# Attention and expert layer on one core: v's blocks turned by the DMA engines instead of TensorE, from the seventh step on

## The chip, the cores and the metric

The kernel runs on one core of a Trainium2 chip. Its engines are TensorE (PE in the profile; PEld is its loading of weights), VectorE (DVE), ScalarE (ACT), GpSimd (POOL) and SyncE (SP), each with an instruction queue of its own that is worked off in order; 16 DMA engines move data between the chip's HBM and the on-chip memory SBUF. Matmuls write to PSUM. The metric is the device time of one execution in microseconds (us), the median of several runs.

## The reference

Four batches of `q`, `k`, `v`, each 5056 tokens by 256 channels in fp32, go through an attention over channels, and all 20224 tokens then through a layer of 8 experts of which each token takes one:

```
qn = q / (norm over tokens + 1e-6);  kn = k / (norm over tokens + 1e-6)
a  = softmax(kn^T @ qn / tau)                     # 256 x 256, one per batch
x  = v @ a                                        # 20224 x 256
e  = argmax(x @ w_gate + modality_bias[modality_id])
p  = the softmax's value at e
out[token] = p * (relu(x[token] @ w1[e]) @ w2[e]) # w1[e] 256 x 1024, w2[e] 1024 x 256
```

## The kernel before, in words

A batch is cut into 10 steps of 512 tokens (the last has 448), so there are 40 steps, numbered g. Per step the kernel does this:

- `va_pieces`: it loads the step's `v` (one transfer of 512 KB, partition p taking four neighbouring tokens), turns it so that channels lie on partitions, splits it in a high part `vh` and a low part `vl`, and multiplies it with the batch's `a` and with `a @ w_gate` in one go (`av`: six matmuls for each of four groups of 128 tokens, tiles `xp`, copied to `x` by ScalarE). `route` works out the expert of each token on VectorE (tiles L, mx, lm, val, vm, oh, run), counts rows per expert by three small matmuls into `rp`, and gives each token a row number; `send` scatters the tokens' rows into the list `xs` in HBM through GpSimd's indirect transfers.
- `kq_pieces`: it loads `q` and `k` of the next batch and adds to that batch's 256 x 256 matrix (matmuls `g`), and sums squares for the norms (tiles `sq`, added to `acc`).
- `block_pieces`: it takes 512 rows of one expert out of `xs` (`xr`), turns them on TensorE (`xtp`), and runs both expert matrices over them (matmuls `hp`, relu into `hh` and its remainder `hl`, matmuls `y`), with weights loaded in halves (`w1r`, `w2r`) and split in high and low parts. The first such block is loaded in step 5 and runs beside step 6; from then on about one block goes with each step, and some are left for after the last step.

Each exact product is made of three matmuls on split operands. All are issued by `_interleave`, which deals the pieces of the three streams out evenly over a step; a scheduler then sets the order on each queue, and pools of buffers (the number of buffers is the number in the pool's name, or `bufs`) decide what has to wait for a release. All plain loads are issued by SP's queue, in order. A transfer on SP waits in that queue until its buffer is free, and whatever is behind it waits too.

The part that the change touches is `tr(h)` (L519 to L531), for each half h of the channels: four transposes on TensorE against the identity `ident` (L524) fill a PSUM tile `vtp`, ScalarE casts it to `vh` (L528), VectorE subtracts to get `vl` (L529). The steps g < 6 are called early; they run before the first block. `first_block` is 6. The pieces `tr(0)`, `tr(1)` of step g + 1 are dealt out at the start of step g, ahead of that step's own `av` and `route`.

Of the kernel before, what the change touches and what calls it, by code (L numbers as in the profile page):

```python
# [8 lines left out]
F32 = mybir.dt.float32  # L9
F32R = mybir.dt.float32r  # L10
BF16 = mybir.dt.bfloat16
I32 = mybir.dt.int32
AF = mybir.ActivationFunctionType
ALU = mybir.AluOpType
# [20 lines left out]
def kernel(  # L35
# [47 lines left out]

    HELD = {1: 3, 2: 2}

    def parts(s):
# [34 lines left out]
        pattern=[[N, B], [STEP, NS], [1, TT]],  # L121
# [92 lines left out]
    def turn_mod():  # L214
# [7 lines left out]
            raw[:R, 0 : 2 * STEP].rearrange("r (p t w) -> r t p w", t=TT, w=2)[:, :, :, 0],  # L222
# [34 lines left out]
    def kq_pieces(b, s, behind=(), later=None):  # L257
# [51 lines left out]
        def square(h):  # L309
            ts = slice(2 * h, 2 * h + 2)  # L310
            a = acc[b]
            for n, o in (("q", 0), ("k", C)):
                first = h == 0 and s == 0
                sq = a[:, :, o : o + C]
                if not first:
# [4 lines left out]
                    if b == 0 or (b == 1 and s < AHEAD):  # L320
                        sq = p3.tile([P, 2, C], F32, tag="hh" if n == "q" else "hl", name=f"sq_{b}_{s}_{h}_{n}")
                    else:
                        sq = p2.tile([P, 2, C], F32, tag="sq", name=f"sq_{b}_{s}_{h}_{n}")
# [36 lines left out]
    def softmax_pieces(b):  # L360
# [27 lines left out]
        def soft(m):  # L388
            rq, rk, ae = st["rq"], st["rk"], st["ae"]
            sc = p1.tile([P, C], F32, tag="sc", name=f"sc_{b}_{m}", bufs=2)  # L390
# [95 lines left out]
    first_block = LAG + START  # L486

    def va_pieces(b, s):
        pp = parts(s)
# [4 lines left out]

        def fetch():
            if "v" in st:
                return
            vt = p2.tile([P, TT, C], F32, tag="v", name=f"v_{g}")
            if pp < P:
                z0 = pp // 32 * 32  # L500
                nc.vector.memset(vt[z0:], 0.0)
            nc.sync.dma_start(
                vt[:pp], v[b, t0 : t0 + pp * TT, :].rearrange("(p t) c -> p t c", t=TT)
            )
            st["v"] = vt

        def load():
            fetch()
# [7 lines left out]
        def tr(h):  # L516
            if early and h == 1:
                tp = ps1.tile([P, 512], F32, tag="y1", name=f"vtp_{g}_{h}")
            else:  # L519
                tp = ps2.tile(  # L520
                    [P, 512], F32, tag="h" if early else "aux", name=f"vtp_{g}_{h}", bufs=2 if early else 3
                )
            for t in range(TT):
                nc.tensor.matmul(  # L524
                    tp[:, t * P : (t + 1) * P], st["v"][:, t, h * P : (h + 1) * P], ident,
                    is_transpose=True, start=t == 0, stop=True, skip_group_check=True,
                )
            cast[g] = nc.scalar.copy(st["vh"][:, h, :], tp).ins  # L528
            ins = nc.vector.tensor_tensor(st["vl"][:, h, :], tp, st["vh"][:, h, :].bitcast(F32), ALU.subtract)  # L529
            if g == 0:  # L530
                order(ins.ins, [i for _, i in weighted])  # L531
# [16 lines left out]
        def route():  # L548
# [19 lines left out]

            W = TT * E
# [6 lines left out]
            else:  # L576
                rp = ps2.tile([P, 512], F32, tag="aux", bufs=3, name=f"rp_{g}")
            nc.tensor.matmul(rp[:, 0:W], trim[:pp], ohf[:pp], start=True, stop=False, skip_group_check=True)
            nc.tensor.matmul(rp[:, 0:W], onesb[:pp], rtf[:pp], start=False, stop=True, skip_group_check=True)
            nc.tensor.matmul(  # L580
                rp[:, W : W + E], onesb[:pp], run_t[:pp, :, TT - 1], start=False, stop=True, skip_group_check=True
# [25 lines left out]
        def send(behind=()):  # L607
            pi, x = st["pi"], st["x"]
            for t in range(TT):
                ins = scatter(  # L610
# [8 lines left out]
            [load] + [lambda h=h: tr(h) for h in range(CH)],  # L619
            [lambda t=t: av(t) for t in range(TT)] + [route],  # L620
            fetch,
# [283 lines left out]
    va = [va_pieces(*divmod(g, NS)) for g in range(G)]  # L905
    run(va[0][0])
# [7 lines left out]
    for g in range(G):  # L914
        b, s = divmod(g, NS)
        streams = []
        if g == first_block - 1:
            va[g + 1][2]()
            va[g + 2][2]()
# [8 lines left out]
        if g - 1 in HELD:  # L928
            t = HELD[g - 1]
            own.insert(t + 1, lambda: va[g - 1][3]([copied[g, t]]))  # L930
        streams.append(soft + (va[g + 1][0] if g + 1 < G else []) + own)
# [107 lines left out]
```

## Time and profile before

| | |
|---|---|
| median of 3 runs | 1235.48 us (1234.66 to 1236.76) |
| the profiled execution's own time | 1232.32 us |
| its span | 1230.5 us |
| mean clock granted to TensorE | 0.996 |
| TensorE busy | 1212.9 us, 99% of the span |
| VectorE busy | 828.8 us, 67% |
| ScalarE busy | 735.6 us, 60% |
| GpSimd busy | 345.6 us, 28% |
| moved by the DMA engines | 210.83 MB, 171 GB/s on average |

The profile shows one execution. Times in it count from the span's start. A line of its groups names the source line, the engine, the operation, out<-in by the tiles' names, the number of instructions, their busy time and the mean length of one; what follows the second bar is the idle time of the engine just before them. In a timeline each row has start, length, engine, line and operation, and in square brackets the idle time before it and what ended that. TensorE's instructions overlap, so the time that one costs is the distance from its start to the next one's start, not its length.

### The profile page before, as it was taken

The page shows a single profiled execution, that of the slowest core. Times are in us where ns is not written, and L with a number is a line of the kernel's source. Part 1 is how long each engine was busy: PE and PEld are TensorE (multiplying, and loading weights), DVE is VectorE, ACT ScalarE, POOL GpSimd, SP SyncE. Part 2 cuts the span into 40 slices and gives each one's busy share as a digit, 9 for nine tenths or more (in the row PEclk, how much of TensorE's full clock was granted, in tenths as well). Part 3 has the DMA queues.
Part 4 walks back from the last instruction along what each step waited for, and adds up shares of the span by engine and source line. Part 5 has one row for each costly group of instructions (what it writes and reads, how often), then busy time and mean ns, then how long its engine had stood idle before and what let it go on. Part 6 is the DMA issues. An engine that isn't in the chain of part 4 may idle for free.

```text
span 1230.5 us, 23793 instructions
## 1 busy us (share of the span) xinstructions
PE 1212.9 (99%) x8368; PEld 1116.1 (91%) x8368; DVE 828.8 (67%) x2182; ACT 735.6 (60%) x1511; POOL 345.6 (28%) x344
## 2 busy tenths in 40 slices
PE   8989999999999999999999999999999999999997
PEld 7888999999999999999999999999999999999996
DVE  6788687877677766776676776666556665575552
ACT  6666676866666665766666665555555555545552
POOL 0061432122322323213222223222222232243121
PEclk9999999999999999999999999999999999999998
DMA  8988555555555655545555564435544554444330
GB/s 306 297 274 281 157 201 171 192 173 174 180 182 173 182 177 174 180 151 181 174 179 184 169 182 147 138 122 154 171 148 142 172 153 138 128 154 146 117 99 29
DMA packets 104177, 210.83 MB, mean 171 GB/s; under 512 B 11336, under 2 KB 52808, under 8 KB 104048
## 3 DMA queue, kind: packets, MB, share of 16 engines
q1 hardware_dynamic: 88304, 167.61, 43.9%
q0 software_dynamic: 15744, 41.61, 9.2%
q8 instruction: 67, 1.10, 0.4%
q14 instruction: 62, 0.51, 0.2%
HBM read 167.06 MB, written 43.43 MB: 171 GB/s over the span
## 4 chain that ended last, share of the span: by engine, by line
PE 86%; issue 7%; DMA 3%; POOL 1%; DVE 1%; ACT 1%; SPq 0%; POOLq 0%; DVEq 0%; ACTq 0%
PE hp L780 32%; PE y L800 32%; PE xp L542 9%; PE g L345 7%; PE vtp L524 3%; PE xtp L761 2%; DMA k<-in_k_dram 2%; POOL out_dram L457 1%; DMA q<-in_q_dram 1%; DMA xs<-x,pi 1%; DMA xr<-xs 0%; PE gw L417 0%; PE ns L367 0%; PE ns L372 0%; SPq L284 0%
## 5 line engine op out<-in xcount | busy, mean ns | idle before, releaser
L800 PE MATMUL y<-w2h,hh 128*128 128x256 f32 x1256 | 355.3, 283 | 0.0
L800 PE MATMUL y<-w2l,hh 128*128 128x256 f32 x1256 | 350.3, 279 | 0.0
L800 PE MATMUL y<-w2h,hl 128*128 128x256 f32 x1256 | 348.7, 278 | 0.1
L457 POOL DMA_INDIRECT out_dram<-yo,xr x158 | 157.2, 995 | 513.3 <-ACT hh L783 400.3
L457 POOL DMA_INDIRECT xs<-x,pi x160 | 175.8, 1099 | 344.4 <-ACT w1h L740 129.1
L784 DVE SCALAR_TENSOR_TENSOR hl<-hp,hh 128x512 fp32r<-128x512 f32 (+1 forms) x320 | 216.4, 676 | 72.5 <-ACT hh L783 72.3
L780 PE MATMUL hp<-xh,w1h 128*128 128x512 f32 (+1 forms) x640 | 255.0, 399 | 0.0
L780 PE MATMUL hp<-xh,w1l 128*128 128x512 f32 (+1 forms) x640 | 250.7, 392 | 0.0
L780 PE MATMUL hp<-xl,w1h 128*128 128x512 f32 (+1 forms) x640 | 250.5, 392 | 0.0
L800 PEld LDWEIGHTS y<-w2h,hh 128*128 128x128 f32 x1256 | 236.0, 188 | 11.0 <-ACT yo L815 0.4
L800 PEld LDWEIGHTS y<-w2l,hh 128*128 128x128 f32 x1256 | 236.5, 188 | 9.6
L783 ACT ACTIVATE hh<-hp 128x512 fp32r<-128x512 f32 (+1 forms) x320 | 190.1, 594 | 83.3 <-PE hp L780 78.0
L800 PEld LDWEIGHTS y<-w2h,hl 128*128 128x128 f32 x1256 | 235.2, 187 | 0.3 <-DVE hl L784 0.3
L747 DVE TENSOR_TENSOR w1l<-w1r,w1h 128x512 fp32r<-128x512 f32 x160 | 110.1, 688 | 173.2 <-ACT w1h L740 171.2
L740 ACT CAST w1h<-w1r 128x512 fp32r<-128x512 f32 x160 | 100.1, 626 | 146.5 <-PE hp L780 143.2
L780 PEld LDWEIGHTS hp<-xh,w1l 128*128 128x128 f32 x640 | 120.5, 188 | 26.2
L780 PEld LDWEIGHTS hp<-xl,w1h 128*128 128x128 f32 x640 | 120.7, 189 | 14.7 <-DVE xl L768 0.4
L780 PEld LDWEIGHTS hp<-xh,w1h 128*128 128x128 f32 x640 | 120.4, 188 | 12.8
L740 ACT CAST w2h<-w2r 128x512 fp32r<-128x512 f32 x160 | 101.2, 632 | 47.9 <-PE y L800 47.7
L747 DVE TENSOR_TENSOR w2l<-w2r,w2h 128x512 fp32r<-128x512 f32 x160 | 109.8, 686 | 23.9 <-ACT w2h L740 21.9
L546 ACT COPY x<-xp 128x264 f32<-128x264 f32 x160 | 61.0, 382 | 81.7 <-PE xp L542 74.6
L542 PE MATMUL xp<-ah,vh 128*128 128x264 f32 x320 | 92.3, 289 | 0.4 <-DVE vl L529 0.4
(153 smaller groups left out, 1712.4 us busy)
## 6 DMA issues: line engine op xcount, KB each, us to landing
w1r<-in_moe_w_dram SPq DMA_DIRECT2D x80, 512.0 KB, 4.1
w2r<-in_moe_w_dram SPq DMA_DIRECT2D x80, 512.0 KB, 3.8
xr<-xs SPq DMA_DIRECT2D x38, 516.0 KB, 4.6
v<-in_v_dram SPq DMA_DIRECT2D x36, 512.0 KB, 3.5
q<-in_q_dram SPq DMA_DIRECT2D x35, 512.0 KB, 6.0
k<-in_k_dram SPq DMA_DIRECT2D x35, 512.0 KB, 6.4
xs<-x,pi POOLq DMA_INDIRECT x160, 5.0
out_dram<-yo,xr POOLq DMA_INDIRECT x158, 3.2
```

Source lines behind the costliest of these rows:

```text
L345: nc.tensor.matmul(gram[b][:, m, :], x, y, start=first and m == 0 and i == 0, stop=last and i == len(seq) - 1, skip_group_check=True,)
L457: ins = nc.gpsimd.indirect_dma_start(out=dst, out_offset=bass.IndirectOffsetOnAxis(ap=idx, axis=0), in_=rows, in_offset=None, bounds_check ...
L524: nc.tensor.matmul(tp[:, t * P : (t + 1) * P], st["v"][:, t, h * P : (h + 1) * P], ident, is_transpose=True, start=t == 0, stop=True, skip ...
L542: nc.tensor.matmul(xp[:, 0:DE], a[:, h, t * P : (t + 1) * P], w[:, h, :], start=i == 0, stop=i == len(seq) - 1,)
L546: copied[g, t] = nc.scalar.copy(st["x"][:, t, :], xp[:, 0:DE]).ins
L740: ins = nc.scalar.copy(hi, src).ins
L747: nc.vector.tensor_tensor(lo, src, hi.bitcast(F32), ALU.subtract)
L761: nc.tensor.matmul(tps[h][:, t * P : (t + 1) * P], st["xr"][:, t, h * P : (h + 1) * P], identr, is_transpose=True, start=t == 0, stop=True ...
L780: nc.tensor.matmul(hp[:, 0:rows], w[:, h, fs], x[:, h, 0:rows], start=i == 0, stop=i == len(seq) - 1)
L783: relu = nc.scalar.activation(hh[:, 0:rows], hp[:, 0:rows], AF.Relu).ins
L784: nc.vector.scalar_tensor_tensor(hl[:, 0:rows], hp[:, 0:rows], 0.0, hh[:, 0:rows].bitcast(F32), ALU.max, ALU.subtract)
L800: ins = nc.tensor.matmul(y, a[:, tsl], w[:, j % 2, :], start=(j == 0 and i == 0 and t % per == 0), stop=(j == NJ - 1 and i == 2), skip_gro ...
```

## The change

From step 6 on, TensorE no longer turns `v`. In its place:

- `fetch` issues one transposing transfer of the step's `v`, read as 16-bit half-words (512 tokens by 512 half-words), from HBM into a tile `T` of 128 partitions by 4 by 512. There is one buffer for `T`. It is issued in step g - 3.
- `halves` sorts the half-words: four transfers from SBUF to SBUF take every other partition of `T` into a tile `pl` of two planes (low half-words, high half-words), 64 partitions by 2 by 512 each. There is one buffer for `pl`. They are issued in step g - 2 (`part`).
- `join`, in step g - 1, builds the fp32 values for each half h in a tile `vt` in SBUF: ScalarE copies the plane of the high half-words and VectorE that of the low ones, each to every other half-word of `vt`. The cast to `vh` and the subtraction to `vl` then read `vt` instead of PSUM.

Around it: the early steps keep the transposes on TensorE, their `v` now in the buffers of `yo`. A partition of a later step holds tokens 128 apart instead of four neighbours, so the table of token numbers (`tokid`), the sorting of the modality bits and the short last step of a batch follow that. The squares of later batches (`sq`) and the softmax's `sc` share three buffers with `vt`; they had two of their own each. The two buffers of `v` are gone, and with them the loading of two later steps' `v` ahead of step 5.

```diff
     def va_pieces(b, s):
-        pp = parts(s)
+        rows = min(STEP, N - s * STEP)
...
+    def halves(T, rows, tag, name):
+
+        out = p1.tile([P, 2, CH, STEP], U16, tag=tag, name=name)
+        if rows < STEP:
+            nc.vector.memset(out[:, :, :, rows:], 0)
+        W = P // 2
+        for w in range(2):
+            for part in range(2):
+                nc.sync.dma_start(out[part * W : (part + 1) * W, w, :, 0:rows], T[w::2, part::2, 0:rows])
+        return out
+
+    def join(dst, src, h):
+
+        both = dst.bitcast(U16).rearrange("p (n w) -> p w n", w=2)
+        nc.scalar.copy(both[:, 1, :], src[:, 1, h, :])
+        nc.vector.tensor_copy(both[:, 0, :], src[:, 0, h, :])
...
         def fetch():
-            if "v" in st:
-                return
-            vt = p2.tile([P, TT, C], F32, tag="v", name=f"v_{g}")
...
+            T = st["T"] = p1.tile([P, 2 * CH, STEP], U16, tag="T", name=f"T_{g}")
+            nc.sync.dma_start_transpose(T[:, :, 0:rows], v.bitcast(U16)[b, t0 : t0 + rows, :])
+
+        def part():
+            st["halves"] = halves(st["T"], rows, "pl", f"pl_{g}")
...
         def tr(h):
-            if early and h == 1:
-                tp = ps1.tile([P, 512], F32, tag="y1", name=f"vtp_{g}_{h}")
+            if h == 0:
+                room()
+            if not early:
+                src = p3.tile([P, STEP], F32, tag="vt", name=f"vt_{g}_{h}")
+                join(src, st["halves"], h)
             else:
...
-            cast[g] = nc.scalar.copy(st["vh"][:, h, :], tp).ins
-            ins = nc.vector.tensor_tensor(st["vl"][:, h, :], tp, st["vh"][:, h, :].bitcast(F32), ALU.subtract)
+            cast[g] = nc.scalar.copy(st["vh"][:, h, :], src).ins
+            ins = nc.vector.tensor_tensor(st["vl"][:, h, :], src, st["vh"][:, h, :].bitcast(F32), ALU.subtract)
...
+            for t in range(TT):
+                if t * P < rows < (t + 1) * P:
+                    nc.vector.memset(oh[rows - t * P :, :, t], 0.0)
...
-        if g == first_block - 1:
-            va[g + 1][2]()
-            va[g + 2][2]()
...
-        streams.append(soft + (va[g + 1][0] if g + 1 < G else []) + own)
+        turn = []
+        if g + 1 < first_block:
+            turn.append(va[g + 1][2])
+        turn += va[g + 1][0] if g + 1 < G else []
+        if first_block <= g + 2 < G:
+            turn.append(va[g + 2][3])
+        if first_block <= g + 3 < G:
+            turn.append(va[g + 3][2])
+        streams.append(soft + turn + own)
```

Three places of the order that the scheduler makes are shown here, before and then with the change. The numbers behind a tile's name only tell its instances apart.

First, VectorE at the end of a step in the last batch, where the routing's chain (L, mx, lm, val, vm, oh, run) runs whose results `oh` and `run` the matmuls `rp` read. Before:

```order
L747 TENSOR_TENSOR w2l_1_13911<-w2r_0_13616,w2h_1_13910 128x512
L551 TENSOR_TENSOR L_13273<-x_13272,bsel_10211 128x32
L553 TENSOR_REDUCE mx_13915<-L_13273 128x4
L555 TENSOR_TENSOR lm_13917<-L_13273,mx_13915 128x32
L559 SCALAR_TENSOR_TENSOR val_13921<-lm_13917,desc 128x32
L563 TENSOR_REDUCE vm_13923<-val_13921 128x4
L597 TENSOR_REDUCE sm_13940<-ex_13919 128x4
L565 TENSOR_TENSOR oh_13925<-val_13921,vm_13923 128x4x8
```

With the change:

```order
L783 TENSOR_TENSOR w2l_1_13955<-w2r_0_13659,w2h_1_13954 128x512
L820 SCALAR_TENSOR_TENSOR hl_6_13927<-hp_6_13919,hh_6_13926 128x512
L560 TENSOR_TENSOR vl_14079<-vt_0_14082,vh_14078 128x512
L582 TENSOR_TENSOR L_13301<-x_13300,bsel_10245 128x32
L515 COPY vt_1_14512<-pl_14131 128x512
L584 TENSOR_REDUCE mx_13970<-L_13301 128x4
L560 TENSOR_TENSOR vl_14079<-vt_1_14122,vh_14078 128x512
L586 TENSOR_TENSOR lm_13972<-L_13301,mx_13970 128x32
L590 SCALAR_TENSOR_TENSOR val_13976<-lm_13972,desc 128x32
L594 TENSOR_REDUCE vm_13978<-val_13976 128x4
L631 TENSOR_REDUCE sm_13995<-ex_13974 128x4
L596 TENSOR_TENSOR oh_13980<-val_13976,vm_13978 128x4x8
```

One subtraction `vl` now stands ahead of the chain, and a copy of the join and the second `vl` stand inside it. On TensorE, the six matmuls `hp_6` now stand ahead of the step's last `xp`, and the six of `hp_7` ahead of `rp`.

Second, ScalarE at the start of the first expert block (slot 0). Before:

```order
L740 CAST w2h_2_1363<-w2r_1_1140 128x512
L528 CAST vh_1340<-vtp_0_1378 128x512
L557 ACTIVATE ex_1209<-lm_1207 128x32
L300 CAST qs_5_0_1410<-q_5_1355 128x2x256
L783 ACTIVATE hh_0_1336<-hp_0_1329 128x512
```

With the change (`pl_1175` holds the planes of step 7):

```order
L588 ACTIVATE ex_1219<-lm_1217 128x32
L776 CAST w1h_2_1374<-w1r_1_1146 128x512
L514 COPY vt_0_1354<-pl_1175 128x512
L776 CAST w2h_2_1378<-w2r_1_1147 128x512
L819 ACTIVATE hh_0_1346<-hp_0_1339 128x512
```

A copy that needs the planes of step 7 now stands ahead of the block's first relu `hh_0`. In the later steps the first join stands between `hh_2` and the cast to `w1h_1`.

Third, SP's queue in a later step. Before:

```order
L700 DMA xr_4461<-xs 128x1032
L284 DMA q_5_5385<-in_q_dram 128x1024
L719 ISA
L719 DMA w1r_0_4885<-in_moe_w_dram 128x2x512
L284 DMA k_5_5387<-in_k_dram 128x1024
L502 DMA v_5368<-in_v_dram 128x1024
```

With the change (another step, of the same batch):

```order
L736 DMA xr_5365<-xs 128x1032
L508 DMA pl_5882<-T_5475 64x2x512 x4
L298 DMA q_7_6299<-in_q_dram 128x1024
L530 DMA_TRANSPOSE T_5922<-in_v_dram 128x4x448
L298 DMA k_7_6301<-in_k_dram 128x1024
L751 TENSOR_LOAD pki_5335
```

The four transfers of `pl` stand right behind `xr`, and the transposing transfer, which waits for all four to have landed because it overwrites the `T` that they read, stands ahead of `k` and of the next weights.

More of the change, by code (lines that the diff above doesn't have):

```diff
@@ L493, in va_pieces, with rows_of_v, room @@
         st = {}
+        def rows_of_v():
+            vt = st["v"] = p2.tile([P, TT, C], F32, tag="yo", name=f"v_{g}")
+            nc.sync.dma_start(vt, v[b, t0 : t0 + rows, :].rearrange("(p t) c -> p t c", t=TT))
         def fetch():
-            if "v" in st:
-                return
-            vt = p2.tile([P, TT, C], F32, tag="v", name=f"v_{g}")
[L499 to L508, printed above, removed]
+            T = st["T"] = p1.tile([P, 2 * CH, STEP], U16, tag="T", name=f"T_{g}")
+            nc.sync.dma_start_transpose(T[:, :, 0:rows], v.bitcast(U16)[b, t0 : t0 + rows, :])
+        def part():
+            st["halves"] = halves(st["T"], rows, "pl", f"pl_{g}")
+        def room():
             st["vh"] = p2.tile([P, CH, STEP], F32R, tag="vh", name=f"vh_{g}")
@@ L516, in tr @@
         def tr(h):
-            if early and h == 1:
-                tp = ps1.tile([P, 512], F32, tag="y1", name=f"vtp_{g}_{h}")
-            else:
[L520 to L529, printed above, removed]
+            if h == 0:
[3 more added lines that the diff above has]
+                join(src, st["halves"], h)
+            else:
+                if h == 1:
+                    src = ps1.tile([P, 512], F32, tag="y1", name=f"vtp_{g}_{h}")
+                else:
+                    src = ps2.tile([P, 512], F32, tag="h", name=f"vtp_{g}_{h}")
+                for t in range(TT):
+                    nc.tensor.matmul(
+                        src[:, t * P : (t + 1) * P], st["v"][:, t, h * P : (h + 1) * P], ident,
+                        is_transpose=True, start=t == 0, stop=True, skip_group_check=True,
+                    )
+            cast[g] = nc.scalar.copy(st["vh"][:, h, :], src).ins
+            ins = nc.vector.tensor_tensor(st["vl"][:, h, :], src, st["vh"][:, h, :].bitcast(F32), ALU.subtract)
             if g == 0:
@@ L567, in route @@
             )
+            for t in range(TT):
+                if t * P < rows < (t + 1) * P:
+                    nc.vector.memset(oh[rows - t * P :, :, t], 0.0)
             W = TT * E
@@ L609, in send @@
             for t in range(TT):
+                pp = min(P, rows - t * P)
                 ins = scatter(
@@ L618, in va_pieces @@
         return (
-            [load] + [lambda h=h: tr(h) for h in range(CH)],
+            [lambda h=h: tr(h) for h in range(CH)],
             [lambda t=t: av(t) for t in range(TT)] + [route],
-            fetch,
+            rows_of_v if early else fetch,
+            part,
             send,
```

31 lines of the change are left out of this document (22 added, 9 removed).

## The prediction

> **What bounds the kernel now.** I read the page's busy times and slices first, then the chain of waits, to see which engine ends last and whether it does so in every stretch.
>
> ```profile
> PE 1212.9 (99%) x8368; PEld 1116.1 (91%) x8368; DVE 828.8 (67%) x2182; ACT 735.6 (60%) x1511; POOL 345.6 (28%) x344
> PE   8989999999999999999999999999999999999997
> PEclk9999999999999999999999999999999999999998
> DMA  8988555555555655545555564435544554444330
> PE 86%; issue 7%; DMA 3%; POOL 1%; DVE 1%; ACT 1%; SPq 0%; POOLq 0%; DVEq 0%; ACTq 0%
> ```
>
> TensorE is busy from the fifth slice on, at its full clock, and 86% of the chain is TensorE. A busy TensorE need not be at its peak, so I read three stretches of busy time by engine (columns: stretch, length, then busy us and count of PE, PEld, DVE, ACT, POOL, granted clock, DMA share, GB/s).
>
> ```profile
> 78.00:94.00 16.00, 12.72 (x91) 10.91 (x89) 12.26 (x55) 10.09 (x27) 10.15 (x11) 0.99 1.01 331
> 94.00:125.00 31.00, 30.97 (x203) 27.65 (x203) 28.54 (x94) 19.12 (x39) 5.88 (x6) 0.95 0.84 273
> 330.00:360.00 30.00, 30.00 (x214) 27.79 (x213) 21.03 (x55) 18.77 (x39) 8.59 (x8) 1.00 0.56 177
> ```
>
> ```profile
> 302.24 0.34 SPq L700 DMA_DIRECT2D xr<-xs  x1
> 332.10 0.34 SPq L700 DMA_DIRECT2D xr<-xs  x1
> ```
>
> At 330 to 360 TensorE never idles, while DVE has 9 us free in 30, ACT 11 us, and the DMA engines 44%. A step lasts 29.9 us there, the distance between two loads of `xr` in the timeline of SP's queue. Only at 78 to 94, ahead of the first expert block, does TensorE stand idle, by 3.3 us, and there the DMA engines are full. So work taken off TensorE in a step after the first block shortens that step by as much, as long as no other queue makes TensorE wait.
>
> **What is removed.** The transposes of 34 of the 40 steps go, 8 in each: 272 of the 320 in the first row. The timeline shows what a block of 8 costs.
>
> ```profile
> L524 PE MATMUL vtp<-ident,v 128*128 128x128 f32 x320 | 43.3, 273 | 0.0
> 343.02 0.28 PE L800 MATMUL y<-w2h,hl 128*128 128x256 f32 x1
> 343.14 1.03 PE L524 MATMUL vtp<-ident,v 128*128 128x128 f32 x8
> 343.93 0.48 PE L780 MATMUL hp<-xh,w1h 128*128 128x512 f32 x1
> 344.25 0.39 PE L780 MATMUL hp<-xl,w1h 128*128 128x512 f32 x1
> 344.48 0.40 PE L780 MATMUL hp<-xh,w1l 128*128 128x512 f32 x1
> ```
>
> From the block's start to the next matmul are 0.79 us, 0.099 a transpose; the mean of 273 ns would count overlapped time. The first `hp` behind it takes 0.32 us to the next start where the following one takes 0.23, so 0.09 us goes on the return from transposes. That makes 0.88 us a step, and 34 x 0.88 = 29.9 us. The lower bound leaves the return out, since another kind of matmul may then bear it: 272 x 0.099 = 26.9 us. I take 29.7, near the upper end, because the view shows the return plainly.
>
> **What is added, off the path.** Per step VectorE and ScalarE each get two copies of 512 half-words; casts and subtractions stay, with another source. The trace has no such copy. The nearest rows:
>
> ```profile
> L226 DVE CAST modlow<-modlow 40x512 f32<-40x512 int32 x1 | 0.4, 419 | 0.0
> L529 DVE TENSOR_TENSOR vl<-vtp,vh 128x512 fp32r<-128x512 f32 x80 | 52.5, 685 | 28.5 <-ACT vh L528 28.4
> L528 ACT CAST vh<-vtp 128x512 fp32r<-128x512 f32 x80 | 44.7, 610 | 3.9 <-PE vtp L524 3.6
> ```
>
> A DVE copy lies between 0.42 us (one source, SBUF to SBUF, the nearest) and 0.69 us (two sources), an ACT copy near 0.61 us. Per step that is 0.8 to 1.4 us on DVE against 9 us free and 1.2 us on ACT against 11 us free: covered on average. Without that cover it would be up to 1.4 us a step, more than the gain. Two places have thin cover, and these are the next two terms.
>
> **The routing's chain.** The matmuls `rp` stand in TensorE's queue and wait for `oh` and `run`. In a step of the last batch:
>
> ```profile
> 924.73 0.28 PE L542 MATMUL xp<-ah,vl 128*128 128x264 f32 x1
> 924.85 0.39 PE L780 MATMUL hp<-xh,w1h 128*128 128x512 f32 x1
> 926.25 0.28 PE L800 MATMUL y<-w2h,hh 128*128 128x256 f32 x1
> 927.65 0.19 PE L578 MATMUL rp<-oh,trim 128*128 128x32 bf16 x1
> 925.05 0.38 ACT L546 COPY x<-xp 128x264 f32<-128x264 f32 x1
> 925.64 0.18 DVE L551 TENSOR_TENSOR L<-x,bsel 128x32 f32<-128x32 f32 x1
> 926.75 0.23 DVE L565 TENSOR_TENSOR oh<-val,vm 128x32 bf16<-128x32 f32 x1
> 927.01 0.22 DVE L573 TENSOR_TENSOR_SCAN run<-keep,oh 128x32 bf16<-128x32 bf16 x1
> ```
>
> The last `xp` starts at 924.73; count from the next matmul, 924.85. Six `hp` take 1.40 us, twelve `y` as much, and `rp` comes at +2.80; `run` ends at +2.38: 0.4 us to spare. With the change `hp_6` moves ahead of that `xp` and `hp_7` ahead of `rp`, in the last batch with three more `y` (0.35 us), so `rp` comes at about +3.15. How VectorE's long instructions follow each other, and what twelve `g` take:
>
> ```profile
> 346.89 0.68 DVE L747 TENSOR_TENSOR w2l<-w2r,w2h 128x512 fp32r<-128x512 f32 x1
> 347.49 0.68 DVE L747 TENSOR_TENSOR w1l<-w1r,w1h 128x512 fp32r<-128x512 f32 x1
> 348.93 1.59 PE L345 MATMUL g<-qs,ks 128*128 128x256 f32 x12
> 350.35 0.28 PE L800 MATMUL y<-w2h,hh 128*128 128x256 f32 x1
> ```
>
> VectorE now does `hl_6` and one `vl` first, 0.6 us from start to start. `hl_6` can begin near +0.07, when the relu of `hp_6` is done, so L starts at about +1.27 instead of +0.79; a copy and the second `vl` inside the chain add 0.7 to 0.95 us (their 0.35 to 0.6 and 0.6, less the 0.25 or so that the chain's own steps wait for each other). `oh` then ends at +3.3 to +3.56, where it ended at +2.13. TensorE waits 0.15 to 0.4 us in each of 8 such steps: 1.2 to 3.3 us, and I take 2. In steps with `g` the twelve `g` (1.42 us) lie in between as well, and one addition to `acc` (0.6) inside the chain: `rp` at about +4.25, `run` at +4.2 to +4.4. I count nothing; 0.15 us in 26 steps, 4 us, is the bound.
>
> **The first blocks.** Here DMA is full and the planes of steps 7 and 8 come late.
>
> ```profile
> 86.72 0.35 SPq L700 DMA_DIRECT2D xr<-xs  x1
> 92.22 0.85 PE L761 MATMUL xtp<-identr,xr 128*128 128x128 f32 x8 [2.80 <-DMA xr<-xs]
> 95.47 0.62 ACT L300 CAST qs<-q 128x512 fp32r<-128x512 f32 x1
> 97.09 0.60 ACT L783 ACTIVATE hh<-hp 128x512 fp32r<-128x512 f32 x1 [1.01 <-PE hp L780]
> DMA to landing us min/median/max: 3.3/4.5/12.0
> ```
>
> The last line is v's load now. Step 7's planes are issued behind the first `xr` (86.72) and one weight load, so at about 88.5, and land by 92 to 100.5. ACT reaches its copy, which stands ahead of the first relu, at about 95.5; behind it wait that relu, then `hl` and TensorE's first `y`. That is 0 to 5 us. Step 8's planes come behind a transposing transfer that itself waits for step 7's planes, and the weights of the second block behind that: once more 0 to 7 us. In the other direction, two `v` loads of 512 KB no longer stand ahead of `xr`, which could give back up to the 2.8 us above. I take a loss of 4, with -3 and 12 as ends.
>
> **SP and the DMA engines.**
>
> ```profile
> 348.90 0.62 ACT L740 CAST w1h<-w1r 128x512 fp32r<-128x512 f32 x1 [0.44 <-PE hp L780]
> ACT w1h L740 <- DMA w1r<-in_moe_w_dram: 3.3, 2, 2.0
> v<-in_v_dram SPq DMA_DIRECT2D x36, 512.0 KB, 3.5
> q1 hardware_dynamic: 88304, 167.61, 43.9%
> ```
>
> The planes are issued right behind `xr` (332.1), in about 2 us, and the first join stands ahead of the cast shown at 348.9: 15 us for a transfer like v's, whose median is 3.5 us. The transposing transfer follows when the planes have landed, near 338, and must have landed when the next planes are issued at 362: 24 us. Behind it on SP wait `k` and the weights, and for these ACT: by the list of waits it has stood only 3.3 us for `w1r` in the whole span, so there is room. Queue q1 spends 0.439 x 1230.5 us of all 16 engines on 167.6 MB, 1.7 us per 512 KB. The planes add 1.7 us a step; the transposing transfer replaces 1.7 by something unseen. Its lower bound is 1.7, its upper one by packets: 98 ns each (0.439 x 1230.5 x 16 / 88304), and were it cut in 256-byte pieces, 2048 of them on 16 engines take 12.5 us. Free are 44% of 29.9, 13.2 us; with 1.7 less and 1.7 more it still fits. I take 1.7 to 4 us and no cost in time.
>
> The Trainium skill speaks against this with one row and for it with another. VectorE: DVE Perf Modes, section "The three transpose paths", gives 1309 ns for a 128x128 16-bit transpose by DMA and advises TensorE; 16 such tiles one after another are an estimated 20.9 us a step, which still lands within the 24 us, so the sum would stay, with 3 us to spare. DMA: Bandwidth & Descriptors, section "Latency and other measured facts", gives 261 GB/s, an estimated 2.0 us. No run so far shows either.
>
> **The sum**, against the profiled execution's 1232.3 us: -29.7 + 2 + 4 = -23.7, so 1208.6 there. That execution lies 3.2 us under the median of the runs, 1235.5; against it the forecast is **1212 us**. Its own ends: 29.9 + 3 gives 1203; 26.9 - 12 - 3.3 - 4 = 7.6 gives 1228, and short of all ends meeting, 1222.
>
> **The rivals.** *The routing takes most of it back.* If ACT's casts or the join hold the chain longer than I count, by 0.3 us in all 34 steps 10 us go, by 0.6 us 20: 1222 to 1232. For it: only 0.4 us to spare now in the last batch, and two more instructions inside. Against: where `g` runs, `rp` comes 1.1 us later. I price it at 1227, with 0.15.
>
> *The transposed load lands late, and it is slower.* Place: ACT's join, with hh queued behind it. It decides from 24 us between issue and landing; from there each us late costs a us in each of 34 steps, less the 0.88 gained. At 26 us: 34 x (2 - 0.88) = +38, so 1274. For it: no such transfer in this trace, and `T` and `pl` have one buffer each, so lateness can't be worked off. Against: v's slowest landing is 12.0 us, in the busiest stretch. Chance 0.15.
>
> *No change*, TensorE being paced by something its busy time hides, or lateness of just 0.9 us: 1235. Against it, the matmul-to-matmul distances in the timeline leave no gaps. Chance 0.05.
>
> **How the numbers follow.** Forecast 0.65, routing 0.15, no change 0.05, late load 0.15. This gives faster by over 0.2% (2.5 us, about what a measurement of this kernel tells from none) 0.80, within 0.05, slower 0.15. The forecast's own range is 1203 to 1222; to hold 8 in 10 the range must take in the routing's case too, so 1203 to 1234.
>
> **What would show it.** Right: `vtp` x48 in the groups; steps of about 29.0 us where they were 29.9; TensorE idle under 0.5 us before `rp`, named DVE; T's landing well under 24 us; the join's idle time on ACT by DMA near zero after 130 us, and a few us between 90 and 125. Wrong: idle time of ACT copies by `pl` in every step; a DMA share near 1.00 in the middle slices; TensorE idle of 0.6 us or more before `rp` in all steps.

## The result, and the profile after

The changed kernel takes 1226.16 us (median of 5 runs, 1224.36 to 1229.32) where the kernel before takes 1234.72 us beside it (1234.27 to 1236.76). The ratio is 0.9931, with a 95% interval of 0.9919 to 0.9943: 8.6 us faster. The forecast was 1212 us, so the change brings here about a third of the 23.7 us that were expected. Measured beside other sets of runs later on, the same kernel took 1221.34 and 1220.74 us, with ratios of 0.9894 (0.9871 to 0.9917) and 0.9908 (0.9891 to 0.9924); the gain is some 9 to 12 us, a third to a half of what was expected.

The page of the changed kernel (its profiled execution took 1226.16 us, its span is 1224.1 us), and three groups of instructions of it:

```profile
PE 1192.0 (97%) x8096; PEld 1089.7 (89%) x8096; DVE 843.2 (69%) x2255; ACT 774.1 (63%) x1579; POOL 351.5 (29%) x345
PE   8998999999999999999999999998999999999996
DMA  8889776677666676478667666436855644444330
PE 76%; issue 8%; DVE 5%; ACT 4%; DMA 4%; POOL 2%; SPq 1%; POOLq 0%; ACTq 0%; DVEq 0%
L514 ACT COPY vt<-pl 128x512 uint16<-128x512 uint16 x68 | 52.7, 785 | 31.5 <-DMA pl<-T 18.1 <-DVE hl L820 6.6 <-issue 3.3
L515 DVE COPY vt<-pl 128x512 uint16<-128x512 uint16 x68 | 31.5, 467 | 13.1 <-DMA pl<-T 11.1 <-issue 1.6
L612 PE MATMUL rp<-oh,trim 128*128 128x32 bf16 x40 | 7.6, 189 | 9.3 <-DVE x L635 4.2 <-DVE oh L596 2.2 <-DVE sm L632 1.5
```

TensorE's busy time fell by 20.9 us (1212.9 to 1192.0), but the span by only 6.4: TensorE is now 97% busy, not 99%, and its share of the chain went from 86% to 76%. The matmuls `rp` alone stood idle for 9.3 us, 4.2 of them at one place. The copies of the join waited for the planes 17 times, 29.2 us in all (18.1 on ScalarE, 11.1 on VectorE).

To see where that falls, I took the start of each step's last `rp` matmul from the timeline. In a step in the middle of a batch (steps 23 to 24 here) and around the start of the last batch (steps 29 to 31):

```profile
634.08 0.17 PE L614 MATMUL rp<-run,onesb 128*128 128x8 bf16 x1
663.04 0.17 PE L614 MATMUL rp<-run,onesb 128*128 128x8 bf16 x1
...
808.16 0.17 PE L614 MATMUL rp<-run,onesb 128*128 128x8 bf16 x1
847.51 0.17 PE L614 MATMUL rp<-run,onesb 128*128 128x8 bf16 x1
872.18 0.17 PE L614 MATMUL rp<-run,onesb 128*128 128x8 bf16 x1
```

The middle step lasts 28.96 us (29.86 before, the same distance): just what was forecast. Steps 30 and 31 last 39.35 and 24.67, together 64.02, where the kernel before takes 57.63. The same matmul in the kernel before:

```profile
816.05 0.17 PE L580 MATMUL rp<-run,onesb 112*128 112x8 bf16 x1
848.52 0.17 PE L580 MATMUL rp<-run,onesb 128*128 128x8 bf16 x1
873.68 0.17 PE L580 MATMUL rp<-run,onesb 128*128 128x8 bf16 x1
```

By stretches, from the `rp` of one step to the `rp` of another, with a saving of 0.88 a step, 4 us lost in the first ten steps and 2 in the last batch as forecast:

| from the rp of step to that of step | before | forecast | measured | off |
|---|---|---|---|---|
| start to 0 | 60.02 | 60.0 | 60.67 | +0.7 |
| 0 to 9 (the first blocks) | 150.36 | 150.8 | 152.80 | +2.0 |
| 9 to 11 (a batch starts) | 64.56 | 62.8 | 66.79 | +4.0 |
| 11 to 19 | 239.21 | 232.2 | 232.72 | +0.5 |
| 19 to 21 (a batch starts) | 62.95 | 61.2 | 62.81 | +1.6 |
| 21 to 29 | 238.95 | 231.9 | 232.37 | +0.5 |
| 29 to 31 (a batch starts) | 57.63 | 55.9 | 64.02 | +8.1 |
| 31 to 39 | 215.22 | 210.2 | 209.80 | -0.4 |
| 39 to the end | 141.60 | 141.6 | 142.12 | +0.5 |

Of the 17.5 us that are missing, 13.7 lie at the three places where a batch starts. The timelines of TensorE, VectorE and ScalarE show what happens at the last of them:

```profile
841.85 0.28 PE L836 MATMUL y<-w2h,hh 128*128 128x256 f32 x1
846.33 0.19 PE L612 MATMUL rp<-oh,trim 128*128 128x32 bf16 x1 [4.19 <-DVE x L635]
841.47 0.16 DVE L632 TENSOR_SCALAR sm<-sm 128x4 f32<-128x4 f32 x1
845.70 0.45 DVE L515 COPY vt<-pl 128x512 uint16<-128x512 uint16 x1 [4.07 <-DMA pl<-T]
846.05 0.22 DVE L596 TENSOR_TENSOR oh<-val,vm 128x32 bf16<-128x32 f32 x1
846.45 1.40 ACT L514 COPY vt<-pl 128x512 uint16<-128x512 uint16 x2 [4.52 <-DMA pl<-T]
```

VectorE is in the middle of step 30's routing: `val`, `vm` and `sm` are done, `oh` is next. But a copy of a join stands ahead of `oh` in its queue, the planes for it are still under way, and VectorE waits 4.07 us for them. `oh` needs none of that; it is just behind. TensorE's `rp` waits for `oh`, 4.19 us, with everything behind it. (The row names L635, which runs right behind `oh` on VectorE and ended last before `rp` by the profile; `rp` reads `oh`.)

Which join is it? Read from the order of the instructions on VectorE's queue (R: the routing of a step, its scan `run`; j: the two copies of a step's join, one letter each; S: the softmax):

```
R22 jj26 R23 jj27 R24 jj28 R25 jj29 R26 jj30 R27 R28 R29 S jj31 jj32 j33 R30 j33 jj34 R31 jj35 R32
```

In the middle of a batch one join stands between two routings, that of the step three or four ahead. Towards a batch's end this lead is used up, because in step 30 the pieces of the softmax are dealt out ahead of the next join. Once the softmax is through, the order catches up: five copies, for three steps, stand between the routings of steps 29 and 30. Each of these joins needs planes of its own, and `pl` and `T` have one buffer each, so their transfers have to run one after the other. The planes of step 31 are there already; those of 32 and 33 have to come in this stretch. SP's timeline:

```profile
824.22 2.58 SPq L508 DMA_DIRECT2D pl<-T  x4
828.54 0.38 SPq L755 DMA_DIRECT2D w1r<-in_moe_w_dram  x1
829.60 2.86 SPq L530 DMA_TRANSPOSE T<-in_v_dram  x1
836.89 0.62 SPq L508 DMA_DIRECT2D pl<-T  x1
837.77 0.40 SPq L759 DMA_DIRECT2D w2r<-in_moe_w_dram  x1
838.63 0.35 SPq L736 DMA_DIRECT2D xr<-xs  x1
839.03 1.92 SPq L508 DMA_DIRECT2D pl<-T  x3
846.49 2.08 SPq L530 DMA_TRANSPOSE T<-in_v_dram  x1
```

The planes of step 32 are sent at 824.22, T for step 33 when they have landed (829.60), and the planes of step 33 when T has landed (836.89): 12.7 us for this round. Weights and rows for the next block are dealt in between the first and the other three of these planes' transfers. They are issued by 841; VectorE's wait ends at 845.70, ScalarE's at 846.45, and the next T, which needs all four to have landed, goes out at 846.49.

The number of copies alone does not set the loss. Between the routings of steps 19 and 20 stand five copies too, and between those of steps 9 and 10 six. `rp` waits 2.16 us in step 10 and not at all in step 20, where a copy on ScalarE waits 0.61 us for planes and none on VectorE. Step 20 is longer than step 30 in the kernel before already (34.50 against 32.47 us), which leaves more time for the rounds; whether that is the reason was not tested.

### The profile page after: what moved, and what is told of

Same layout as the page of the kernel before. It is cut to its first block, busy times and chain, and to the rows that moved or that the text cites. A ratio compares the mean times of both kernels' runs of the same rounds, so it can differ in the third digit from the quotient of the medians.

```text
span 1224.1 us, 23572 instructions
## 1 busy us (share of the span) xinstructions
PE 1192.0 (97%) x8096; PEld 1089.7 (89%) x8096; DVE 843.2 (69%) x2255; ACT 774.1 (63%) x1579; POOL 351.5 (29%) x345
## 4 chain that ended last, share of the span: by engine, by line
PE 76%; issue 8%; DVE 5%; ACT 4%; DMA 4%; POOL 2%; SPq 1%; POOLq 0%; ACTq 0%; DVEq 0%
PE y L836 29%; PE hp L816 28%; PE g L359 9%; PE xp L573 8%; DMA pl<-T 2%; PE xtp L797 2%; POOL out_dram L471 1%; DVE vl L560 1%; DMA k<-in_k_dram 1%; ACT hh L819 1%; ACT yo L851 1%; ACT vh L559 1%; DMA T<-in_v_dram 1%; DVE hl L820 0%; DMA xr<-xs 0%
## 5 line engine op out<-in xcount | busy, mean ns | idle before, releaser
L471 POOL DMA_INDIRECT xs<-x,pi x160 | 181.8, 1136 | 444.7 <-issue 142.5
L816 PE MATMUL hp<-xh,w1h 128*128 128x512 f32 (+1 forms) x640 | 251.2, 393 | 0.5 <-DVE hl L820 0.5
L573 PE MATMUL xp<-al,vh 128*128 128x264 f32 x320 | 92.0, 288 | 0.0
```

Of the source, the lines that this page charges most:

```text
L471: ins = nc.gpsimd.indirect_dma_start(out=dst, out_offset=bass.IndirectOffsetOnAxis(ap=idx, axis=0), in_=rows, in_offset=None, bounds_check ...
L573: nc.tensor.matmul(xp[:, 0:DE], a[:, h, t * P : (t + 1) * P], w[:, h, :], start=i == 0, stop=i == len(seq) - 1,)
L816: nc.tensor.matmul(hp[:, 0:rows], w[:, h, fs], x[:, h, 0:rows], start=i == 0, stop=i == len(seq) - 1)
```

## The experiments

The expectations call it theory A that the copies stand in the queue ahead of the routing. Its rivals are that the transfers as such are too slow (B), the shared buffers (C), and the softmax standing ahead of the transfers (D). Theory E (catching up) and A' are later forms of A and D.

**The copies behind the routing.** Each copy of the join for step g is put behind the routing of step g - 2 on its own queue; the planes' and T's transfers, issued behind it, follow.

```diff
-        nc.scalar.copy(both[:, 1, :], src[:, 1, h, :])
-        nc.vector.tensor_copy(both[:, 0, :], src[:, 0, h, :])
+        hi = nc.scalar.copy(both[:, 1, :], src[:, 1, h, :]).ins
+        lo = nc.vector.tensor_copy(both[:, 0, :], src[:, 0, h, :]).ins
+        for ins, on in ((hi, "act"), (lo, "dve")):
+            order(ins, [i for n, i in routed[g - 2] if n == on])
```

> The copies of the join for step g are put, on their own queues, behind the routing of step g - 2; nothing else is changed. Theory A (the queue's order): in the changed kernel the copies for up to three steps stand between one routing and the next where a batch begins, and VectorE waits there for planes that are still under way, with the routing's chain behind it. Then this run wins back the wait of 4.2 us before rp in step 30, the 2.2 us in step 10, and the 0.2 to 0.8 us before rp in the last batch, with some lateness behind them: 7 to 10 us, so 1216 to 1219 us. Theory B (the transfers are too slow): the planes are just as late, another instruction waits for them, and the time stays within 2 us of 1226. Theory C (vt's buffers shared with the squares and the softmax): as B.

Measured: 1213.21 us (1212.70 to 1213.91), ratio 0.9837 (0.9821 to 0.9853). The three batch starts last 63.31, 61.74 and 55.97 us, within 0.6 us of the forecast of the table; VectorE's copies never waited for a transfer, ScalarE's 0.2 us. That is 13 us under the first measurement of the changed kernel and 8 us under the later ones, where A expected 7 to 10; the changed kernel was not measured beside this run. B and C are out, which expected no gain: the transfers, their sizes and the shared buffers are the same. It has a price too: most steps in the middle of batches last 29.3 us, not 28.96. In these steps six `hp` take 1.56 us instead of 1.38 and the twelve `y` behind them 1.55 instead of 1.41. TensorE's weight load for the first of these `y` waits for ScalarE's `yo`:

```profile
640.14 0.19 PEld L838 LDWEIGHTS y<-w2h,hh 128*128 128x128 f32 x1 [0.44 <-ACT yo L853]
638.21 1.14 ACT L561 CAST vh<-vt 128x512 fp32r<-128x512 f32 x2
639.24 1.57 ACT L853 ACTIVATE yo<-y,xr 128x256 f32<-128x256 f32 x4
```

The join's two casts to `vh` now stand right ahead of `yo` on ScalarE. In the whole run the weight loads of `y` wait 8.1 us for `yo`, in the changed kernel 2.0. Steps 18 and 19 pay more, 30.34 and 32.76 us instead of 29.1 each: a `y` waits 1.92 us for `yo` there, and ScalarE has stood 5.9 us for a load of `k`. So the stretch from step 11 to 19 is 5.4 us longer than in the changed kernel.

**The join ahead of the softmax.**

```diff
-        streams.append(soft + turn + own)
+        streams.append(turn + soft + own)
```

> In steps 10, 20 and 30 the join of the next step and the two transfers behind it are dealt out ahead of the softmax instead of behind it. Theory A: the copies of the steps after that still stand ahead of the routing of steps 10, 20 and 30, since nothing holds them back, so it is worth 0 to 4 us: 1222 to 1226. Theory D (the planes are late at the batch's start because the softmax stands ahead of their transfers): the loss at the three batch starts, about 13 us against 0.88 us saved per step, goes for the most part: 1214 to 1217.

Measured: 1211.60 us (1210.40 to 1212.37), ratio 0.9826 (0.9809 to 0.9842). This is D's side, and A's 0 to 4 us was wrong. The batch starts last 62.98, 61.56 and 57.08 us, 1.8 us over the forecast in all. In the order, three to five copies still stand between the two routings at a batch's start, but their transfers were asked for earlier: T for step 13 goes out 11.3 us after the `rp` of step 9 (223.22 against 211.90), in the changed kernel 21.5 us after it (234.95 against 213.47). First this run, then the changed kernel:

```profile
223.22 1.98 SPq L530 DMA_TRANSPOSE T<-in_v_dram  x1
```

```profile
234.95 4.51 SPq L530 DMA_TRANSPOSE T<-in_v_dram  x1
```

No `rp` waits there by more than 0.04 us. So a copy ahead of the routing does harm only where its planes are late. The two theories are not rivals but two halves of one cause.

**Three joins in a step without a softmax.** To part "the softmax's steps" from "catching up", the order behind the routing was set only for steps 12 to 15, 22 to 25 and 32 to 35. This moves the catching up to steps 14, 24 and 34:

```
R9 S jj11 R10 jj12 R11 jj13 R12 jj14 R13 jj15 jj16 jj17 R14 jj18 R15
```

> The copies of the join are put behind the routing of step g - 2 only for the second to fifth step of each later batch. In the order, the three joins that stood between two routings where a batch begins then stand there four steps later, between the routings of steps 13 and 14, 23 and 24, 33 and 34, where there is no softmax. Theory E (catching up: whenever three joins stand between two routings, three rounds of planes and transposing transfers, one after the other, have to fit in one step): steps 10, 20 and 30 are 3 to 9 us shorter, and steps 14, 24 and 34 are longer by 5 to 10 us each; in all 1220 to 1236. Theory A' (it is the softmax of these steps that makes the copies come in the way): the loss goes and does not come back, 1213 to 1217.

Measured: 1221.78 us (1219.61 to 1223.76), ratio 0.9903 (0.9886 to 0.9920). Against the changed kernel of the same set (1221.34) nothing is gained, as E says. The batch starts are 1.7, 0.6 and 8.6 us shorter; the steps 14 and 15, 24 and 25, 34 and 35 together are 4.9, 2.9 and 4.8 us longer, and steps 12, 22 and 23 are 0.3 us longer each. TensorE, and VectorE, where the moved wait now is in the last batch:

```profile
948.61 0.21 PE L614 MATMUL rp<-oh,trim 128*128 128x32 bf16 x1 [2.96 <-DVE sm L634]
941.96 0.47 DVE L515 COPY vt<-pl 128x512 uint16<-128x512 uint16 x1 [5.84 <-DMA pl<-T]
```

The same wait for planes, of the same kind, in a step that has no softmax. The sizes were over-rated (5 to 10 us were expected each).

**Half of the planes' transfers.** If late planes are the price, lighter planes must lower it. Only the high half-words are moved, and both copies read them; the low half of each v is thus other bits. x changes a little, some tokens take another expert, and four more blocks run at the end (8704 matmuls, not 8096), so the total (1343.14 us) says nothing; the steps up to 39 compare.

```diff
-        for w in range(2):
+        for w in (1,):
...
-        nc.vector.tensor_copy(both[:, 0, :], src[:, 0, h, :])
+        nc.vector.tensor_copy(both[:, 0, :], src[:, 1, h, :])
```

> Only the plane of the high half-words is moved; the join reads it twice, so the low half of each v is other bits and the result is off in the third digit. All instructions of the engines stay, the order puts six copies of three joins between the routings at a batch's start as before, and half of the transfers between SBUF and SBUF is gone. Theory E with the transfers' time as the price: the wait before rp in step 30, 3.9 to 4.3 us, shrinks to under 2 and steps 10, 20, 30 get 2 to 6 us shorter in sum, 4 us or more in all. If only the copies' place in the queue counts, the wait stays and the time too.

Beside it, the changed kernel itself:

> The changed kernel once more, to stand beside the next two on one chip, since its runs have lain between 1217 and 1229 us. Steps 10, 20 and 30 again 38 to 39, 36 and 39 us long; 1217 to 1226 us.

Measured: in the changed kernel (1220.74 us, 1220.66 to 1222.71) `rp` of step 30 waits 4.11 us, with half the planes 1.47. First the changed kernel, then the one with half of the planes:

```profile
841.41 0.19 PE L612 MATMUL rp<-oh,trim 128*128 128x32 bf16 x1 [4.11 <-DVE x L635]
```

```profile
836.77 0.19 PE L612 MATMUL rp<-oh,trim 128*128 128x32 bf16 x1 [1.47 <-DVE x L635]
```

Steps 30 and 31 take 58.39 us, not 63.26; the first batch start gains 1.1 us, the second loses 0.3. This sum of 5.7 us fits E, but it does not prove it alone. Six copies for three joins stand ahead of the routing of step 30, one more than in the changed kernel, so the place in the queue alone would not have made it better; yet nearly all of the gain comes from this start, where the order differs, and VectorE still waits 3.54 us for planes there (3.99 in the changed kernel), only earlier. At the other two starts, where the order is the same, the gain is 1.1 and -0.3. All the waits of the join's copies for planes together fall from 33.7 to 8.8 us.

**T by a plain transfer.** In place of the transposing transfer, one of the same 512 KB that does not transpose; the join reads every other half-word.

```diff
-            nc.sync.dma_start_transpose(T[:, :, 0:rows], v.bitcast(U16)[b, t0 : t0 + rows, :])
+            nc.sync.dma_start(T, v.bitcast(U16)[b, t0 + rows - STEP : t0 + rows, :].rearrange("(p t) c -> p t c", t=TT))
```

> T is filled by a plain transfer of the same 512 KB, as v's was before the change, instead of the transposing one; the planes, the copies of the join, the cast and the subtraction have the same sizes, but read words in pairs. v is thus left unturned, so x holds other numbers of the same kind. Theory B (the transposing transfer is late or takes the others' bandwidth): 8 to 11 us faster than the changed kernel, 1215 to 1218, with the planes landing earlier. Theory A: the order on the queues is nearly the same, the planes land some 2 to 4 us sooner after their issue, so a part of the wait in step 30 goes: 1 to 4 us faster, 1222 to 1225.

Here too x, the experts and with them the last blocks differ (8704 matmuls, 1341.07 us), so only the steps count. Step 30 takes 33.35 us and its `rp` does not wait; the wait, 1.45 us, has moved to the `rp` of step 31. The order differs there by one copy: four copies, not five, stand ahead of the routing of step 30. The first batch start keeps its length (64.49). From issue to landing the plain transfer takes 4.3 us (the median of the 8 whose landing the profile shows). For the transposing one the profiles of six runs show 28 landings, 4.1 to 9.4 us after the issue, with a median near 6; the lowest and the highest median of those runs with more than two landings are 4.8 and 6.6. First the plain one, then these two:

```profile
T<-in_v_dram SPq DMA_DIRECT2D x34, 512.0 KB, 4.3
```

```profile
T<-in_v_dram SPq DMA_TRANSPOSE x31, 4.8
```

```profile
T<-in_v_dram SPq DMA_TRANSPOSE x34, 6.6
```

By these medians the transposing transfer lands 0.5 to 2.3 us later than the plain one, far from the 24 us at which it would decide. What it adds, at a batch's start, comes on top of the chain of rounds; since the order differs too, this run does not tell the two apart.

**The routing's term by itself.** The set order only for steps 34 to 39.

> The same fence only for steps 34 to 39. It prices the routing's term by itself: the steps 32 to 38 of the last batch last 26.54 us in the changed kernel and should last 26.1; 0.4 us in 5 to 6 steps, 2 to 3 us in all: 1223 to 1224. If the copies inside the routing's chain cost nothing, no difference.

Measured: 1215.95 us (1212.83 to 1219.67), ratio 0.9867 (0.9838 to 0.9896). From step 31 to 39 it takes 207.12 us, the changed kernel of the same set 209.32: 2.2 us, as expected for this stretch, though the total was expected at 1223 to 1224. Most of these steps last 26.10 us, where steps 32 to 34 of the changed kernel last 26.5, and `rp` no longer waits. The rest of the difference between the two profiled executions (1212.8 and 1219.7 us) lies where the two kernels are alike, 2.4 us in the first ten steps (150.05 against 152.48) and 2.4 at the batch starts: executions differ there by as much as this term.

**The first blocks.** In one run the transposes of steps 6 to 8 stay on TensorE (their v in the buffers of `T` and `pl`); in another all steps are changed, with the set order for steps 6 to 9 only.

> Steps 6, 7 and 8 stay with the transposes on TensorE (their v lies in the buffers of the planes and of T, loaded two at once in step 5, as before the change); the new way begins with step 9. If the first blocks lose about 6.5 us because planes compete with the first weights and rows, this gives back 6.5 and costs 3 x 0.88 = 2.6: 4 us faster, 1222. If the loss there has nothing to do with the planes (v's early loads, the other buffers), it is 2.6 us slower: 1229.

> The fence only for the joins of steps 6 to 9, so that no copy for the steps ahead stands before the routing of steps 4 to 7 or ahead of the first block's relu. If the loss at the first blocks comes from copies that wait in front of the first relu, as the prediction had it, steps 5 to 9 get 2 to 4 us shorter against the changed kernel of this set, and nothing changes after step 10. If the loss is the DMA engines' being full while rows and weights of the first two blocks are loaded, it stays within 1.5 us.

Measured: 1217.35 us (1216.97 to 1219.27, ratio 0.9877, 0.9860 to 0.9893), and 1216.15 us (1213.79 to 1218.02, ratio 0.9863, 0.9843 to 0.9882). From step 0 to 9 they take 151.2 and 150.2 us, the changed kernel beside the second 153.8: 2.6 and 3.6 us less, the first of these although it saves 2.6 us less of transposes (steps 5 to 9 of the second alone are 1.9 us shorter, between the two expected cases). One execution each does not settle the size: with the changed kernel's order in these steps the run of the last paragraph took 150.05 us, as little as the better of these two. What repeats is a wait. In all seven profiles that have this order and the transposing T, TensorE waits a second time for rows, 1.2 to 4.5 us, at `xtp` of the second block. In the three with the order set early (this one, the one with the order set everywhere and the last one below) and in the one that keeps TensorE's transposes up to step 8, it does not. So the new transfers, in this order, make that wait. SP's timeline, TensorE's and ScalarE's of the changed kernel, then of the one with the order set early, then the second `xr` of the kernel before:

```profile
88.66 2.88 SPq L508 DMA_DIRECT2D pl<-T  x4
96.76 3.40 SPq L530 DMA_TRANSPOSE T<-in_v_dram  x1
100.43 0.40 SPq L755 DMA_DIRECT2D w1r<-in_moe_w_dram  x1
102.88 0.36 SPq L736 DMA_DIRECT2D xr<-xs  x1
109.08 0.49 PE L797 MATMUL xtp<-identr,xr 128*128 128x128 f32 x2 [3.56 <-DMA xr<-xs]
97.92 0.59 ACT L819 ACTIVATE hh<-hp 128x512 fp32r<-128x512 f32 x1
```

```profile
104.05 0.34 SPq L738 DMA_DIRECT2D xr<-xs  x1
113.23 0.80 PE L799 MATMUL xtp<-identr,xr 128*128 128x128 f32 x8
```

```profile
96.49 0.34 SPq L700 DMA_DIRECT2D xr<-xs  x1
```

The transposing transfer waits in SP's queue for the planes to land, and the weights and rows of the second block wait behind it: `xr` goes out at 102.88, where the kernel before had sent it at 96.49, and TensorE stands 3.56 us. With the order set early the second `xr` is no earlier (104.05), but TensorE comes to its `xtp` only at 113.23, with the other work ahead of it, and does not wait; in the changed kernel it stood there from 105.5. The copy ahead of the first relu, which the prediction named first, is the smaller part: it waits 1.41 us for planes, and the relu is 0.8 us later than before (97.92 against 97.09).

**The changed kernel again.**

> The changed kernel, as it is, for a second profiled execution. In the first one TensorE lost 3.3 us in step 2, before any transfer of the new kind was used. If that belongs to one execution, step 2 is 7.2 to 7.5 us long here, while steps 10 and 30 again last some 39 us; if it belongs to the change (v in the buffers of yo), it is there again.

Measured: 1221.34 us (1216.97 to 1221.65). Step 2 lasts 7.16 us, so 3 us of the loss of the first execution in the first ten steps were its own. The batch starts last 64.95, 62.15 and 64.54 us, and the first blocks 152.48 in all: against the forecast of the table the loss at the batch starts is 11.8 us here and 5.6 at the first blocks. In the third execution (the one beside half of the planes) they are 9.4 and 6.9. The loss at the batch starts is there each time, but its size differs from execution to execution by 4 us.

**A version that beats both.** The join ahead of the softmax, and the set order for steps below 13 and from 31 on.

```diff
-                join(src, st["halves"], h)
+                join(src, st["halves"], h, routed[g - 2] if g < 13 or g >= 31 else ())
...
-        streams.append(soft + turn + own)
+        streams.append(turn + soft + own)
```

> The join ahead of the softmax in steps 10, 20 and 30, and the fence for steps below 13 and from 31 on, where it shortened steps, but not in between, where it lengthened them by 0.3 us (29.28 against 28.96). By adding the stretches of the two runs: 1.3 us from the first ten steps, 2 to 3 us from the last batch against the run with the join ahead of the softmax alone: 1207 to 1209. If the two act on the same loss, 1211.

Measured: 1208.17 us (1205.89 to 1211.21), ratio 0.9800 (0.9776 to 0.9823). That is 24.8 us under the kernel before of that set (1233.01) and 13.2 under the changed one. The same cut into stretches, from step 0 to 9 on, gives 150.66, 64.23, 231.98, 61.56, 231.99, 55.78 and 207.47 us.

## Why the prediction was wrong

- **What is removed** was right: 0.88 us a step was forecast, and the steps in the middle of batches went from 29.86 to 28.96. The lower bound, without the return from the transposes, was not needed.
- **SP and the DMA engines at no cost, as an average:** right in the middle steps, wrong where several rounds fall in one step. The prediction worked out 15 us for the planes and 24 us for T from steps in which everything runs evenly. A bound worked out in an even step says nothing of a step in which the order catches up.
- **The failed step is the one that the sum does not have: the start of a batch.** The change was followed from the first blocks to the middle of batches to the last batch, and nothing was counted for steps 10, 20 and 30, where the softmax stands ahead of the join. They cost 13.7, 11.8 and 9.4 us in three executions, in place of nothing: copies for three steps stand there ahead of one routing, their planes come one round after the other, and TensorE's `rp` waits for VectorE's `oh` behind them, up to 4.2 us. The run with the order set everywhere and the one with the join first both take this loss away; the one that moves the catching up moves the loss. The one with half the transfers lowers it, but with another order at the place where it gains. The prediction's own sign failed at the same place: ScalarE's copies were to wait near nothing for planes after 130 us, and waited 15 us.
- **The routing's chain:** 2 us was forecast, 2.2 measured by itself, at the place and of the size worked out (0.44 us a step in the last batch, nothing in steps with `g`, where `rp` never waits in the middle of batches). At the batch starts it is the same place, TensorE's `rp` behind VectorE's `oh`, with a stall of 4 us instead of 0.4: the rival "the routing takes most of it back" named the place but priced a copy's own length, not what the copy waits for.
- **The first blocks:** 4 us was forecast; the loss was 3 us in the first execution (without what step 2 lost there), 5.6 in the second and 6.9 in the third (153.80, against 150.36 less 3.5), within the ends of -3 and 12. Of its two halves the second weighs more: T waits for the planes, with the second block's weights and rows behind it, and TensorE waits for those rows (1.2 to 3.6 us in these three), where the first relu is late by 0.8.
- **The rivals:** the transposed load does not land late: the landings that the profiles show come 4.1 to 9.4 us after the issue, not 24, and the steps keep their new length. Its second ground, that `T` and `pl` with one buffer each can't work off lateness, was however what counted at the batch starts. The Trainium skill's figure in VectorE: DVE Perf Modes, section "The three transpose paths" (1309 ns a tile, an estimated 20.9 us a transfer one tile after the other) is not what this transfer takes.

With these losses taken out, the kernel lies at 1208.17 us; against a kernel before of 1233.01 the forecast sum of -23.7 gives 1209.3. That the two meet is partly luck: this version also takes out the routing's 2 us, which the forecast had counted, so by its own terms it should lie 2 us lower. The middle of the forecast was sound, the places where streams meet were not in it.

## What to carry to other kernels

A load or copy that is moved ahead on an in-order queue is only as harmless as its data is early: look for the places where the order catches up (the start of a batch, the end of a phase), and count there how many rounds of a single-buffered transfer have to fit, and what stands behind the waiting copy. An average of free time over even steps does not cover them. What holds the work back can be as little as where pieces are dealt out: one line (the join ahead of the softmax) was worth as much as the order of all joins (1211.60 and 1213.21 us).

## What the runs showed of the hardware

**A wait of TensorE costs more than its length.** Windows of 5 us of the changed kernel around the wait of step 30 (columns: stretch, length, busy us and count of PE, PEld, DVE, ACT, POOL, granted clock, DMA share, GB/s):

```profile
840.00:845.00 5.00, 2.13 (x13) 1.72 (x11) 1.63 (x7) 1.18 (x2) 0.00 (x0) 1.00 0.82 244
845.00:850.00 5.00, 3.67 (x15) 2.89 (x16) 3.35 (x19) 1.77 (x3) 0.75 (x1) 0.71 0.46 107
850.00:855.00 5.00, 5.00 (x35) 4.62 (x34) 2.72 (x6) 3.42 (x8) 3.78 (x5) 0.95 0.57 140
855.00:860.00 5.00, 5.00 (x35) 4.61 (x34) 1.99 (x3) 2.49 (x5) 1.98 (x2) 1.00 0.99 265
```

After the wait the granted clock falls for a short time; 0.29 and 0.05 of 5 us each are 1.7 us of full clock lost, behind a wait of 4.2. In the profiles of eight runs of the kernels above there are eleven waits of TensorE of 1.9 us or more past 200 us. Nine come with such a dip: seven of 1.7 us, and two of 3.4 us that begin before the wait ends, so that some 0.8 us of each falls into it. Two waits (2.27 and 2.95 us) have none, nor has any of the eight between 1.0 and 1.7 us. The Trainium skill, TensorE: Matmul & The Clock Gate, section "Part 1: The HAM clock gate", has the clock halved for a free-running window of about 3.4 us after one that was idle; half of 3.4 is the 1.7 us seen here, but five waits of 1.9 to 3.0 us, shorter than such a window, were enough for it. So the wait at the start of the last batch cost nearly 6 us.

**The transposing transfer moves its data in small packets.** The pages before and after:

```profile
DMA packets 104177, 210.83 MB, mean 171 GB/s; under 512 B 11336, under 2 KB 52808, under 8 KB 104048
```

```profile
DMA packets 188563, 228.40 MB, mean 187 GB/s; under 512 B 82664, under 2 KB 141544, under 8 KB 188432
q1 hardware_dynamic: 172752, 185.19, 52.6%
```

There are 71328 more packets under 512 bytes. If all belong to T, that is 2098 for each of the 34 transfers of up to 512 KB, or about 250 bytes a packet. The queue q1 takes 0.526 x 1224.1 - 0.439 x 1230.5 = 103.7 us of all 16 engines more, 3.05 us a step, for planes and T together. If the planes take the 1.7 us of other transfers of their size, T takes an estimated 1.7 + 3.05 - 1.7 = 3.05 us, far below the 12.5 us that the prediction had worked out as the upper end for such packets.

**Half-word copies:** 467 ns on VectorE and 785 ns on ScalarE for 512 half-words that land in every other place. VectorE's lies in the range of the prediction, ScalarE's above the 0.61 us taken from its cast.
